# Attention and MoE on one core: where chunk 0's shifted V comes from, and the order of the first loads

## The chip, the cores and the metric

The kernel runs on one core of one Trainium2 chip. The metric is the device time of one execution in microseconds. Before the change the median of eight runs is 252.09 us (251.44 to 253.89). All other times in this document are from one profiled execution of the kernel, counted from the start of its span.

## The reference

Attention with two kinds of heads, followed by a two-layer network with a leaky ReLU:

```python
batch, n_heads, seq, head_dim = (4, 8, 768, 64)
n_sink, window = (4, 64)
is_retrieval = [1, 0, 1, 0, 0, 0, 1, 0]
n_tokens, d_model, d_ff = (3072, 512, 2048)

scores = scale * np.matmul(q, k.transpose(0, 1, 3, 2))
rel = pos[:, None] - pos[None, :]
causal = rel >= 0
stream_keep = causal & (is_sink | ((rel >= 0) & (rel < window)))
mask = full causal for retrieval heads, stream_keep for the others
a = softmax of the masked scores
attn_out = np.matmul(a, v)
x = attn_out, heads side by side           # 3072 x 512
h = x @ w_in
g = np.maximum(0.01 * h, h)
out = g @ w_out
```

Three heads of eight see the whole past. The other five ("stream" heads) see the last 64 keys and four first keys ("sinks").

## The kernel before

The 4 x 768 tokens are worked in eight chunks of 384; chunk n is batch n // 2, half n % 2. Each chunk goes through three stages: attention (class `Attention`, L289), the first matrix with the leaky ReLU (`in_slots`, L460, 16 slots of four matmuls), and the second matrix (`out_slots`, L472). `merge` (L503) lays the slots of one chunk's attention between matrix slots of the chunk before, and the order so written is the order in which every engine executes: nothing reorders it later. TensorE, ScalarE, VectorE, POOL and SP each run their own list in order, and meet at semaphores.

**Loads.** q, k, v and both weight matrices are float32 in DRAM and bfloat16 on the chip. A load that changes the type is issued by POOL (`load`, L78; `load_w`, L95). So POOL carries one long list of casting loads: q of chunk 0 (three), the identity matrix, v of chunk 0 (three), the masks (`masks`, L143), four loads of the first weights, then k, q and v of chunk 1, four loads of the second weights, and k, q, v of chunk 2 and on. The built program gives these loads eight completion semaphores in turn, so that each waits, on POOL, for the load eight places before it to have landed. k of chunk 0 comes by SP, without a cast.

**k and q with the head's width in the partitions.** Chunks 0 and 1 are transposed on TensorE (`prep_first`, L239; `prep_pair`, L205). From chunk 2 on SP issues six DMA transposes for each chunk (`prep_dma`, L228: `kt` from `kz` at L235, `qt` from `qb` at L237). SP's list in order is: shift of V for chunk 1, transposes of chunk 2, three stores of chunk 0's output, shift of V for chunk 2, transposes of chunk 3, and so on. Chunk 2's first score reads all of `qt`.

**Shifted V.** A stream head's query block of 64 needs 128 keys that begin 64 before it, so its V is read from `vb`, which holds V moved by 64 tokens. In most chunks SP makes `vb` from `va` by two DMA copies (`v_shift`, L176). In chunk 0 TensorE does it: `v_shift_pe` (L184) multiplies `va` with two shift matrices, four matmuls of 455 columns into the banks "py" and "pt", and ScalarE and VectorE copy one result each. `late_constants` (L157) builds the shift matrices and the mask of the stream heads, inside `prep_first`, ahead of the copy of q.

**Banks.** PSUM has eight banks: two "ph", two "psS", two "po", one "py", one "pt" (L55). A pair of heads accumulates in a "po" bank until VectorE has divided it (`finish`, L402); the result goes through a transpose bank (`x_t`, L417). An output tile of `out_slots` takes "py", which is free again when VectorE has copied it.

**The start** (L516 to L558) issues the loads, runs chunk 0's attention with `v_shift_pe` between slots 6 and 7, then seven in-slots of chunk 0, the four TensorE preparations of chunk 1 with an in-slot behind each, and the merge of the remaining in-slots and the out-slots of chunk 0 with chunk 1's attention.

Of the kernel before, what the change touches and what calls it, by code (L numbers as in the profile page):

```python
# [11 lines left out]
FP32 = mybir.dt.float32  # L12
BF16 = mybir.dt.bfloat16
ACTF = mybir.ActivationFunctionType
# [7 lines left out]
def kernel(  # L22
# [12 lines left out]
    nc = tc.nc  # L35
    B, H, S, D = q.shape
# [20 lines left out]
    def bank(tag, shape, dtype):  # L57
        return ps.tile(shape, dtype, name=tag, tag=tag, bufs=BANKS[tag])
# [19 lines left out]
    def load(n, nms="kqv"):  # L78

        b, c = divmod(n, 2)  # L80
        for nm in nms:
            if nm == "k" and n >= BY_DMA:

                for g in range(3):
                    for hh in range(2):
                        nc.gpsimd.dma_start(out=kz[n % 2][:, g, hh::2, D * hh : D * hh + D],  # L86
                                            in_=nat[nm][b, c, :, hh::2, g])
                continue
            if nm != "v":
                cast[nm, n] = rot.tile([128, 3, H, D], BF16, name=f"{nm}b", tag=f"{nm}b", bufs=2)  # L90
            for g in range(3):
                o = va[b % 2][:, 3 * c + g, :, 0:D] if nm == "v" else cast[nm, n][:, g]
                nc.gpsimd.dma_start(out=o, in_=nat[nm][b, c, :, :, g])  # L93

    def load_w(which, i):  # L95

        if which == "in":
            c = slice(512 * i, 512 * i + 512)
            nc.gpsimd.dma_start(out=w_in_bf[:, :, c], in_=w_in_r[:, :, c])
        else:  # L100
            c = slice(4 * i, 4 * i + 4)
            nc.gpsimd.dma_start(out=w_out_bf[:, c, :], in_=w_out_r[:, c, :])
# [5 lines left out]
    def bf(name, *shape):  # L108
        return one.tile([128, *shape], BF16, name=name)

    ident = bf("ident", 128)
    m_caus = bf("m_caus", 128)
    m_win0 = bf("m_win0", 6, 64)
    shift = bf("shift", 2, 128)
    kt = [bf(f"kt{i}", 4, 2, S) for i in range(2)]
    va = [bf(f"va{i}", 6, H, D + 1) for i in range(2)]
    vb = [bf(f"vb{i}", 5, H, D + 1) for i in range(2)]
# [25 lines left out]
    def masks():  # L143
        nc.gpsimd.memset(m_caus[:], 1.0)
        keep(m_caus[:], [[1, 128]], ALU.is_ge, 0, -1)
        nc.gpsimd.memset(m_w[:], 1.0)
        keep(m_w[:], [[-1, 64]], ALU.is_gt, 0, 1)
        keep(m_w[:], [[1, 64]], ALU.is_ge, 64, -1)

        nc.gpsimd.memset(m_h[:], 1.0)  # L150
        keep(m_h[:], [[-NS, H]], ALU.is_ge, 0, 1)
        keep(m_h[:], [[NS, H]], ALU.is_ge, NS - 1, -1)
# [2 lines left out]
        return ap.rearrange("p (o r) -> p o r", o=1).to_broadcast([128, n, w])  # L155

    def late_constants():  # L157

        nc.vector.tensor_copy(shift[:, 0, 0:64], ident[:, 64:128])
        nc.vector.tensor_copy(shift[:, 1, 64:128], ident[:, 0:64])  # L160
        nc.vector.tensor_copy(m_win0[:, 1:], spread(m_w[:], 5, 64))
        nc.vector.tensor_copy(m_win0[:, 0, :], m_caus[:, 0:64])
        nc.vector.memset(m_win0[0:NS, 1, :], 1.0)
        for h in range(H):
            if IS_RETR[h]:
                nc.vector.memset(m_h[:, h : h + 1], 0.0)
# [14 lines left out]
        eng.dma_start(out=vb[i][0:64, lo:hi], in_=va[i][64:128, lo:hi])  # L181
        eng.dma_start(out=vb[i][64:128, lo:hi], in_=va[i][0:64, lo + 1 : hi + 1])

    def v_shift_pe():  # L184

        w = 7 * (D + 1)
        for t in range(2):
            p = bank(("py", "pt")[t], [128, 512], FP32)
            for e in range(2):
                nc.tensor.matmul(p[:, 0:w], lhsT=shift[:, e, :], rhs=va[0][:, t + e, 1:H, :],  # L190
                                 start=(e == 0), stop=(e == 1))
            src = p[:, 0:w].rearrange("p (h d) -> p h d", h=7)
            if t == 0:
                nc.scalar.activation(out=vb[0][:, t, 1:H, :], in_=src, func=ACTF.Copy)
            else:
                nc.vector.tensor_copy(vb[0][:, t, 1:H, :], src)

    def sink_keys(n, p, hh):
        b, c = divmod(n, 2)
# [39 lines left out]
    def prep_first():  # L239

        k0 = stage["k"].rearrange("p h (g d) -> p g h d", g=3)
        qts[0] = rot.tile([128, 4, CH], BF16, name="qt", tag="qt", bufs=2)
        nc.vector.tensor_copy(cast["k", 0][:, :, 0:4], k0[:, :, 0:4])
        nc.scalar.activation(out=cast["k", 0][:, :, 4:8], in_=k0[:, :, 4:8], func=ACTF.Copy)
        pts = {}
        for nm, half, tag in (("k", 0, "pt"), ("k", 1, "py"), ("q", 0, "po"), ("q", 1, "po")):
            pt = pts[nm, half] = bank(tag, [128, 2, 4, 128], BF16)
            if nm == "q":
                continue
            for e in range(2):  # L250
                p = 2 * half + e
                for g in range(3):
                    nc.tensor.transpose(pt[:, e, g, :], cast[nm, 0][:, g, 2 * p : 2 * p + 2, :], ident[:])
        for g in range(3):
            for p in range(4):
                nc.tensor.transpose(pts["q", p // 2][:, p % 2, g, :], cast["q", 0][:, g, 2 * p : 2 * p + 2, :], ident[:])
        tok = lambda ap: ap.rearrange("p e (t g) -> p e t g", g=3)

        def k_rows(half, hh, act=False):
            ps2 = slice(2 * half, 2 * half + 2)  # L260
            r = slice(64 * hh, 64 * hh + 64)
            src = pts["k", half][r, :, 0:3, :].rearrange("p e g t -> p e t g")
            dst = tok(kt[0][r, ps2, hh, 0:CH])
            if act:
                nc.scalar.activation(out=dst, in_=src, func=ACTF.Copy)
            else:
                nc.vector.tensor_copy(dst, src)

        def q_rows(half):
            return (qts[0][:, 2 * half : 2 * half + 2, :].rearrange("p e (g t) -> p e g t", g=3),  # L270
                    pts["q", half][:, :, 0:3, :])

        k_rows(0, 0)
        k_rows(0, 1)
        k_rows(1, 0, True)
        k_rows(1, 1)
        for h in range(H):
            sink_keys(0, h // 2, h % 2)
        late_constants()
        d, r = q_rows(0)  # L280
        nc.scalar.activation(out=d, in_=r, func=ACTF.Copy)
        d, r = q_rows(1)
        nc.vector.tensor_copy(d, r)
# [174 lines left out]
    py = {}  # L458
# [13 lines left out]
    def out_slots(n, tags=("py", "py", "py"), halves=False):  # L472
        slots = []

        def part(tt, lo, hi, tag, c0, c1):
            if lo == 0:
                py[n] = bank(tag, [128, 512], FP32)
            for ng in range(lo, hi):
                nc.tensor.matmul(py[n][:, 0 : c1 - c0], lhsT=gs[n][:, ng, 128 * tt : 128 * tt + 128],  # L479
                                 rhs=w_out_bf[:, ng, c0:c1], start=(ng == 0), stop=(ng == NG - 1))  # L480
            if hi == NG:
                o = rot.tile([128, DM], FP32, name="o", tag="o", bufs=3)
                r0 = CH * n + 128 * tt
                nc.vector.tensor_copy(o[:, 0 : c1 - c0], py[n][:, 0 : c1 - c0])  # L484
                nc.sync.dma_start(out=out[r0 : r0 + 128, c0:c1], in_=o[:, 0 : c1 - c0])

        for tt in range(3):
            if halves and tt == 2:
                slots.append(lambda: part(2, 0, NG, "py", 0, 256))
                slots.append(lambda: part(2, 0, NG, "psS", 256, 512))  # L490
                continue
            lo = 0
            for w in ([3, 3, 3, 3, 4], [3, 3, 3, 3, 4], [3, 3, 3, 3, 2, 2])[tt]:
                slots.append(lambda tt=tt, lo=lo, w=w: part(tt, lo, lo + w, tags[tt], 0, DM))
                lo += w
        return slots

    def run(*lists):
        for l in lists:
            for f in l:  # L500
                f()

    def merge(ms, as_):  # L503

        r, done = [], 0
        for j, m in enumerate(ms):
            want = (j + 1) * len(as_) // len(ms)
            r += as_[done:want] + [m]
            done = want
        return r + as_[done:]  # L510
# [10 lines left out]
            nc.scalar.dma_start(out=sv[NS * h : NS * h + NS], in_=v[:, h, 0:NS, :].rearrange("b r d -> r b d"))  # L521
    for t in va:
        nc.vector.memset(t[:, :, :, D], 1.0)
    nc.vector.memset(shift[:], 0.0)
    zeros(0, 0)
    nc.vector.memset(ksink[0][:], 0.0)
    load(0, "v")
    masks()
    for i in range(4):
        load_w("in", i)  # L530
    load(1)
    for a in ats:
        nc.vector.memset(a[:, :, 1:3, :], 0.0)
    for i in range(4):
        load_w("out", i)
    prep_first()
    a0 = Attention(0, ("psS", "ph"), x_tags=("pt", "py")).slots(order=[0, 2, 1, 3, 4, 5, 6, 7], LAG=4, XLAG=3, sink_after={0, 2})
    run(a0[0:6])
    sink_values(0)
    v_shift_pe()  # L540
    run(a0[6:])
    zeros(0, 1)
    nc.vector.memset(ksink[1][:], 0.0)
# [2 lines left out]
    in0 = in_slots(0, ("ph", "psS"))  # L546
# [5 lines left out]
    prep_dma(2)  # L552

    a1 = Attention(1, po_tags=("po", "po", "po", "ph")).slots(order=[0, 2, 6, 1, 3, 4, 5, 7])
    run(merge(in0[11:], a1[:8]) + merge(out_slots(0), a1[8:]))
    zeros_k(1)
    v_shift(2, nc.sync)
    load(3)  # L558
# [58 lines left out]
```

The softmax here doesn't subtract the row's maximum and nothing guards it: scores larger than these inputs give would overflow.

## Time and profile before

| | |
|---|---|
| median of the runs | 252.09 us |
| profiled execution | 251.44 us, span 249.6 us |
| TensorE matmuls (PE) busy | 228.8 us, 92% |
| ScalarE (ACT) busy | 137.1 us, 55% |
| VectorE (DVE) busy | 86.7 us, 35% |
| POOL busy | 79.8 us, 32% |
| POOL's casting loads, as a share of 16 DMA engines | 70.8% |
| SP's and ScalarE's loads, copies, transposes and stores, the same share | 35.4% |

A row of the timeline gives start, length, engine (a "q" behind it means the engine's list of instructions that issue DMAs), line, operation, tile written <- tiles read, shape and count; in square brackets stands how long the engine sat idle before it, and what ended that. TensorE is busy in most of the span, but the idle time is not spread evenly: the start has nearly all of it. A row of DMA gives the issue; when the data landed is told beside it.

### The profile page before, as it was taken

Reading aid. Unit: us, or ns where it says so; the run is one execution under the profiler, and the core shown is the slowest. Engines: PE = TensorE matmul, PEld = TensorE weight load, DVE = VectorE, ACT = ScalarE, POOL = GpSimd, SP = SyncE. Lnnn points to the kernel's source line nnn. Section 1 sums busy time; section 2 is a strip of 40 time slices with the busy share of each in tenths; the row PEclk is TensorE's granted clock in tenths of the full one; section 3 lists DMA queues with packets and bytes.
Section 4 is the critical chain, followed back from the end, with each engine's and each line's share of the span. In section 5 each row is a group of like instructions: output and inputs, shape, how many; then the busy total and the mean of one; then the engine's idle time right before and its main releaser. Section 6 shows DMA issues by size and latency. Waiting matters only on the chain.

```text
span 249.6 us, 5031 instructions
## 1 busy us (share of the span) xinstructions
PE 228.8 (92%) x2012; PEld 138.5 (56%) x2012; DVE 86.7 (35%) x250; ACT 137.1 (55%) x297; POOL 79.8 (32%) x109
## 2 busy tenths in 40 slices
PE   1787799986999999989999999999999999999994
PEld 0564455553665567555665566566655566545553
DVE  6976141165235324323421323433521251111121
ACT  2665357433882298856556677556557667433300
POOL 8973833976437482385271000000000000000000
PEclk9999899999999999999999999999999999999999
DMA  9999999999999999999999921196100100111012
GB/s 163 125 204 180 166 234 181 138 166 189 213 135 160 184 200 139 162 120 151 197 169 194 135 67 42 49 146 145 45 27 19 42 20 25 42 45 42 28 56 87
DMA packets 110971, 30.14 MB, mean 121 GB/s; under 512 B 101732, under 2 KB 107108, under 8 KB 110948
## 3 DMA queue, kind: packets, MB, share of 16 engines
q0 software_dynamic: 76272, 13.24, 70.8%
q1 hardware_dynamic: 34576, 16.56, 35.4%
q8 instruction: 16, 0.26, 0.4%
q14 instruction: 7, 0.06, 0.1%
q10 hardware_dynamic: 100, 0.02, 0.0%
HBM read 27.28 MB, written 6.29 MB: 135 GB/s over the span
## 4 chain that ended last, share of the span: by engine, by line
PE 66%; DMA 22%; POOL 4%; SPq 3%; issue 2%; ACT 1%; DVE 1%; POOLq 0%
PE ph L466 26%; PE py L479 23%; DMA qb<-in_q_dram 8%; DMA qt<-qb 7%; DMA va<-in_v_dram 4%; PE po L308 4%; PE psS L341 4%; PE psS L479 3%; DMA w_in_bf<-in_moe_w_in_dram 3%; SPq L235 2%; POOL qb L93 2%; PE psS L377 2%; PE psS L466 1%; POOL va L93 1%; PE pt L420 1%
## 5 line engine op out<-in xcount | busy, mean ns | idle before, releaser
L466 PE MATMUL ph<-xt,w_in_bf 128*128 128x384 bf16 x480 | 97.2, 328 | 0.1
L479 PE MATMUL py<-w_out_bf,g 128*128 128x512 bf16 (+1 forms) x336 | 87.2, 374 | 1.5 <-DVE o L484 1.2
L468 ACT ACTIVATE g<-ph 128x384 bf16<-128x384 f32 x120 | 59.0, 492 | 49.2 <-PE ph L466 48.6
L466 PEld LDWEIGHTS <-w_in_bf 128*128 128x128 bf16 x512 | 45.9, 98 | 29.3 <-issue 1.5
L479 PEld LDWEIGHTS <-g 128*128 128x128 bf16 x400 | 35.7, 97 | 28.6 <-issue 2.9
L346 ACT ACTIVATE at<-psS 128x384 bf16<-128x384 f32 x81 | 39.2, 492 | 15.4 <-PE psS L341 14.3
L86 POOL DMA_DIRECT2D kz<-in_k_dram x36 | 26.8, 759 | 28.7 <-DMA kt<-kz 10.3
L341 PE MATMUL psS<-qt,kt 128*128 128x384 bf16 (+2 forms) x104 | 26.5, 295 | 2.6 <-DMA qt<-qb 2.2
L484 DVE COPY o<-py 128x512 f32<-128x512 f32 (+1 forms) x21 | 14.2, 677 | 40.4 <-PE py L479 40.2
L93 POOL DMA_DIRECT2D qb<-in_q_dram x24 | 21.3, 893 | 15.4 <-DMA va<-in_v_dram 8.0
L93 POOL DMA_DIRECT2D va<-in_v_dram x24 | 21.2, 897 | 6.9 <-DMA w_in_bf<-in_moe_w_in_dram 4.7
L382 ACT ACTIVATE ats<-psS 128x384 bf16<-128x384 f32 x38 | 18.8, 495 | 6.1 <-PE psS L377 6.0
L421 ACT ACTIVATE xt<-pt 128x384 bf16<-128x384 bf16 x30 | 14.7, 489 | 11.2 <-PE pt L420 10.7
L308 PE MATMUL po<-va,at 128*128 128x65 bf16 x237 | 20.3, 196 | 0.3 <-DVE at L350 0.3
L308 PEld LDWEIGHTS <-at 128*128 128x128 bf16 x252 | 16.4, 99 | 6.9 <-DVE at L350 0.7
L414 DVE TENSOR_TENSOR xs<-po,linv 128x384 bf16<-128x384 f32 x31 | 17.3, 558 | 1.1
L352 DVE TENSOR_TENSOR at<-at,m_caus 128x128 bf16<-128x128 bf16 x24 | 5.4, 225 | 34.5 <-ACT at L346 34.5
L341 PEld LDWEIGHTS <-kt 128*128 128x128 bf16 x108 | 10.5, 100 | 11.7 <-issue 4.9
L350 DVE TENSOR_TENSOR at<-at,m_caus 128x256 bf16<-128x256 bf16 x24 | 7.0, 291 | 24.4 <-ACT at L346 24.4
L377 PEld LDWEIGHTS <-kt 128*128 128x128 bf16 x240 | 12.1, 100 | 5.8 <-issue 0.7
L308 PE MATMUL po<-va,ats 128*128 128x65 bf16 x137 | 12.9, 194 | 1.1 <-DVE xs L414 1.1
L308 PEld LDWEIGHTS <-ats 128*128 128x128 bf16 x240 | 11.5, 98 | 3.9 <-DVE xs L414 1.2
(94 smaller groups left out, 176.2 us busy)
## 6 DMA issues: line engine op xcount, KB each, us to landing
out_dram<-o SPq DMA_DIRECT2D x23, 256.0 KB, 3.0
qb<-in_q_dram POOLq DMA_DIRECT2D x24, 128.0 KB, 8.1
va<-in_v_dram POOLq DMA_DIRECT2D x24, 128.0 KB, 10.2
kz<-in_k_dram POOLq DMA_DIRECT2D x36, 64.0 KB, 10.7
w_in_bf<-in_moe_w_in_dram POOLq DMA_DIRECT2D x4, 512.0 KB, 8.2
w_out_bf<-in_moe_w_out_dram POOLq DMA_DIRECT2D x4, 512.0 KB, 12.0
vb<-va SPq DMA_DIRECT2D x8, 195.0 KB, 5.9
vb<-va SPq DMA_DIRECT2D x6, 130.0 KB, 4.1
```

Of the source, the lines that this page charges most:

```text
L86: nc.gpsimd.dma_start(out=kz[n % 2][:, g, hh::2, D * hh : D * hh + D], in_=nat[nm][b, c, :, hh::2, g])
L93: nc.gpsimd.dma_start(out=o, in_=nat[nm][b, c, :, :, g])
L308: nc.tensor.matmul(o, lhsT=lhsT, rhs=rhs, start=first, stop=False, skip_group_check=True)
L341: nc.tensor.matmul(s[:, off : off + w], lhsT=kt[i][:, p, hh, 128 * kj : 128 * kj + 128], rhs=qts[n][:, p, lo:CH], start=(j == 0), stop=(j ...
L346: nc.scalar.activation(out=a[:, 0:off], in_=s[:, 0:off], func=ACTF.Exp, scale=SM)
L377: nc.tensor.matmul(s[:, 64 * m : 64 * m + 64], lhsT=kt[i][:, p, hh, k0 : k0 + 128], rhs=qts[n][:, p, 64 * m : 64 * m + 64], start=(m == 0) ...
L382: nc.scalar.activation(out=av_, in_=s[:, 0:CH].rearrange("p (j e f) -> p j e f", j=3, e=2), func=ACTF.Exp, scale=SM)
L414: nc.vector.tensor_tensor(xs[:], po[:, :, :, 0:D], linv.to_broadcast([128, 3, 2, D]), op=ALU.mult)
L421: nc.scalar.activation(out=xts[self.n][:, p, :], in_=pt[:, 0, 0:3, :], func=ACTF.Copy)
L466: nc.tensor.matmul(ph[:, 0:CH], lhsT=w_in_bf[:, g, 128 * t : 128 * t + 128], rhs=xts[n][:, g, :], start=(g == 0), stop=(g == KG - 1))
L468: nc.scalar.activation(out=gs[n][:, t, :], in_=ph[:, 0:CH], func=ACTF.Prelu, alpha=0.01)
L479: nc.tensor.matmul(py[n][:, 0 : c1 - c0], lhsT=gs[n][:, ng, 128 * tt : 128 * tt + 128], rhs=w_out_bf[:, ng, c0:c1], start=(ng == 0), stop= ...
```

## The change

Four things are changed, all of them in the first two chunks:

- `v_shift_pe` and its shift matrices are gone. `load_vb0` loads the first two blocks of chunk 0's shifted V from DRAM by two casting loads on POOL, behind v and ahead of the masks. Their column of ones is set by one memset, in place of the one that cleared the shift matrices.
- Chunk 0's attention uses "py" as a third accumulator bank (pair 2), and "pt", "ph", "psS", "pt" for its transposes. Chunk 0's out-slots use "py", "ph", "py".
- `late_constants` is called behind the first four slots of chunk 0's attention.
- k and q of chunk 1 are loaded ahead of the fourth load of the first weights; v of chunk 1 stays behind it.

```diff
-    shift = bf("shift", 2, 128)
...
     def late_constants():
-
-        nc.vector.tensor_copy(shift[:, 0, 0:64], ident[:, 64:128])
-        nc.vector.tensor_copy(shift[:, 1, 64:128], ident[:, 0:64])
         nc.vector.tensor_copy(m_win0[:, 1:], spread(m_w[:], 5, 64))
...
-    def v_shift_pe():
...
+    def load_vb0():
+
         for t in range(2):
...
+            nc.gpsimd.dma_start(out=vb[0][:, t, :, 0:D],
+                                in_=v[0, :, 128 * t + 64 : 128 * t + 192, :].rearrange("h p d -> p h d"))
...
             sink_keys(0, h // 2, h % 2)
-        late_constants()
         d, r = q_rows(0)
...
-    nc.vector.memset(shift[:], 0.0)
+    nc.vector.memset(vb[0][:, 0:2, :, D], 1.0)
     zeros(0, 0)
     nc.vector.memset(ksink[0][:], 0.0)
     load(0, "v")
+    load_vb0()
     masks()
-    for i in range(4):
+    for i in range(3):
         load_w("in", i)
-    load(1)
+    load(1, "kq")
+    load_w("in", 3)
+    load(1, "v")
...
-    a0 = Attention(0, ("psS", "ph"), x_tags=("pt", "py")).slots(order=[0, 2, 1, 3, 4, 5, 6, 7], LAG=4, XLAG=3, sink_after={0, 2})
-    run(a0[0:6])
+    a0 = Attention(0, ("psS", "ph"), po_tags=("po", "po", "py", "po"),
+                   x_tags=("pt", "ph", "psS", "pt")).slots(order=[0, 2, 1, 3, 4, 5, 6, 7], LAG=4, XLAG=3, sink_after={0, 2})
+    run(a0[0:4])
+    late_constants()
+    run(a0[4:6])
     sink_values(0)
-    v_shift_pe()
     run(a0[6:])
...
-    run(merge(in0[11:], a1[:8]) + merge(out_slots(0), a1[8:]))
+    run(merge(in0[11:], a1[:8]) + merge(out_slots(0, ("py", "ph", "py")), a1[8:]))
```

## The prediction, made before the changed kernel was run

> **What bounds the kernel now.** I read the page's chain and busy shares first, then the TensorE groups that sat idle, then the queues that the chain names (SP and POOL), and last the granted clock by stretches of 3.4 us. TensorE's rows with idle time before them, for the stretch 60 to 130 us, are only four:
>
> ```profile
> 61.39 0.32 PE L341 MATMUL psS<-qt,kt 128*128 128x384 bf16 x1 [1.45 <-DMA qt<-qb]
> 102.68 0.27 PE L308 MATMUL po<-va,at 128*128 128x65 bf16 x3 [0.30 <-DVE at L350]
> 104.75 0.34 PE L420 MATMUL pt<-ident,xs 128*128 128x128 bf16 x3 [0.23 <-DVE xs L414]
> 107.16 0.32 PE L341 MATMUL psS<-qt,kt 128*128 128x384 bf16 x1 [0.77 <-DMA qt<-qb]
> ```
>
> From 61.39 us to the end TensorE stands still for 0.30 + 0.23 + 0.77 = 1.3 us. So the end is set by when chunk 2's first score (61.39) may start, plus TensorE work that this change leaves alone. That score waits for a DMA, not for TensorE: SP's queue shows the six transposes of chunk 2 (start, issue time),
>
> ```profile
> 43.53 1.37 SPq L235 DMA_TRANSPOSE kt<-kz  x1
> 46.11 1.19 SPq L237 DMA_TRANSPOSE qt<-qb  x1
> 47.41 1.49 SPq L235 DMA_TRANSPOSE kt<-kz  x1
> 49.00 1.78 SPq L237 DMA_TRANSPOSE qt<-qb  x1
> 50.88 2.73 SPq L235 DMA_TRANSPOSE kt<-kz  x1
> 53.70 1.42 SPq L237 DMA_TRANSPOSE qt<-qb  x1
> ```
>
> and the chain follows the last for 7.55 us, to 61.25. The first needs two kz loads; those were issued at 29.13 and 30.19 and took 13.9 and 13.3 us to land: 43.0 and 43.5. They are late because POOL's queue is full ahead of them: the page's DMA row is at nine tenths or more from the start to slice 23. POOL's own rows show where that queue begins:
>
> ```profile
> 4.62 2.75 POOL L93 DMA_DIRECT2D va<-in_v_dram  x3
> 7.34 0.24 POOL L144 MEMSET m_caus<- 128x128 bf16 x1
> ...
> 8.77 0.45 POOL L128 TENSOR_SCALAR_AFFINE_SELECT m_h<-m_h 128x8 bf16<-128x8 bf16 x2
> 9.16 3.01 POOL L99 DMA_DIRECT2D w_in_bf<-in_moe_w_in_dram  x4
> ```
>
> The bound of the front, then, is POOL's queue of casting loads -> kz and q of chunk 2 -> transposes -> 61.39. TensorE's own work before 61 us has slack: it was done at 61.39 - 1.45 = 59.94.
>
> **The change, part by part.**
>
> *Two loads of shifted V on POOL, ahead of the masks.* They have the shape of the va loads (128 partitions x 8 heads x 64 values). The nearest row is L93, va<-in_v_dram, 897 ns of POOL each: 2 x 0.897 = 1.79 us. Behind them on POOL stand the masks and every later load. Masks first: m_caus is ready at 7.95 + 1.79 = 9.7, needed at about 11 by the first mask product; m_w and m_h at about 11, needed by the moved constants later still. Nothing is lost there. Then the weights: the first w_in load goes from 9.16 to 10.95. It took 5.6 us to land (14.74), the next three landed at 17.25, 19.8 and 23.3 (7.3, 9.1 and 11.9 us after issue). From there the queue has no gap until w_out has landed, so all that stands behind w_in, kz of chunk 2 included, shifts by 1.79.
>
> Here a rule speaks for a smaller number. The Trainium skill, "DMA: Bandwidth & Descriptors", section "Anatomy of one DMA — SWDGE (gpsimd) path", puts a software-queue transfer at a fixed 2.0 us of completion plus bytes/436e3; the fixed part overlaps in a full queue, so two loads of 256 KB read would cost 2 x 0.6 = 1.2 us. The rows here disagree: three va loads took 2.75 us of POOL, and chunk 1's three q loads reached TensorE at 27.11, 28.01 and 28.89, 0.9 us apart. By the rule the shift is 1.2, by the rows 1.8. I take the rows, and keep 1.2 as the lower end.
>
> *k and q of chunk 1 ahead of the fourth w_in load.* TensorE stood still for q three times (to 27.11, 28.01, 28.89). The fourth w_in load held the queue from 19.8 to 23.3 = 3.5 us, so the last q lands at 28.84 + 1.79 - 3.5 = 27.1, a gain of 1.7 us at that place. The fourth w_in load then lands at about 30.6; its first user (in-slot 12) ran at 36.0. v of chunk 1, w_out and kz have the same loads ahead of them as before plus two: +1.79. Nothing of the gain reaches them.
>
> *V shift taken off TensorE.* Four 455-column matmuls from 13.21 to 14.71 go (1.5 us), with one ScalarE copy of 0.55 us and one VectorE cast of 0.63. In their place the first vb product waits for the loads: issued at about 7.4 and 8.2, with the 5.1 us that va loads took they land at 12.5 and 13.4; the first use stood at 15.91 and may come at 14. Wait 0 to 0.5 us. The vb ones memset replaces the shift memset (0.17 us): nothing.
>
> *Constants later, third bank.* VectorE's constants (10.69 to 11.55, 0.86 us) now stand behind four mask products; chunk 0's second q copy comes 0.9 earlier, which the 0.26 us wait at 12.17 pays back. The bank "py" for pair 2 removes the wait of 1.09 us at 17.93. Together TensorE is through chunk 0 some 2 to 3 us earlier (21.4 -> about 18.7), and all of it is lost to the wait for q at 27.1.
>
> *What TensorE makes of it up to 61 us.* It leaves the q wait 1.7 us earlier. Next in its way is w_out: the four loads landed at 33.7, 37.8, 40.0 and 42.6 (8.0, 11.4, 12.6, 14.3 us after issue), now 1.79 later; the last, 44.4, is needed by the out-slot that started at 44.85 and would now start at 43.1. So 0.5 us of the gain is left. Chunk 0's output banks py, ph, py instead of py alone remove the two waits for the output copy (0.53 at 46.66, 0.68 at 53.29): 1.2 us. TensorE is done with what it can do at 59.94 - 0.5 - 1.2 = 58.2. The gate comes at 61.25 + 1.79 = 63.0. Everything saved on TensorE becomes idle time there: 4.8 us where it was 1.45. **The start of chunk 2 moves by +1.8 us.**
>
> *The granted clock.* The price of such a gap is in the trace of before (columns: stretch, length, busy us of PE, PEld, DVE, ACT and POOL, granted PE clock, DMA share, GB/s):
>
> ```profile
> 25.51:28.93 3.42, 1.56 (x12) 0.79 (x11) 0.00 (x0) 1.10 (x3) 3.11 (x5) 1.00 2.43 155
> 28.93:32.34 3.41, 3.41 (x17) 2.07 (x18) 2.13 (x6) 0.49 (x1) 2.51 (x5) 0.50 1.54 193
> 59.65:63.06 3.41, 1.97 (x14) 1.10 (x13) 2.24 (x9) 1.48 (x4) 1.81 (x3) 1.00 1.60 241
> ```
>
> After a stretch with 1.56 us of TensorE in 3.42 the clock was halved for 3.41 us, which costs 1.7 us of dense matmuls; after one with 1.97 us it was not. The Trainium skill, "TensorE: Matmul & The Clock Gate", Part 1, says that the clock falls to half after an idle window of about 3.4 us, the windows running free of the program. Read literally, a 4.8 us gap holds a whole window in (4.8 - 3.4)/3.4 = 4 of 10 phases: 0.4 x 1.7 = 0.7 us. The row shows that a window half idle, with a few transposes in it, is enough; with 4.8 us some window is at least 2.4 us idle in any phase. I take the row: one window, +1.7 us (0, or up to 3 where a second window is needed to rise again, are the ends).
>
> *What is given back.* Chunk 4's transposes start behind chunk 1's output copies on SP, so behind TensorE, and move with it; but the loads they compete with do not wait for the cold clock, so half of the 0.77 us at 107.16 may go: -0.4.
>
> Sum: 1.8 + 1.7 - 0.4 = **+3.1 us**. The profiled execution took 251.44 us (span 249.6 and 1.84 around it), the fastest of eight; it becomes 254.5. The median of the runs, 252.09, becomes **255.2 us**.
>
> **Rivals.**
>
> *Gate late, clock kept.* The gap is shorter than I think (w_out later, TensorE later), or falls well in the windows. +1.8: 253.9. For it: the gap at 61.39 was not punished before. Against: all TensorE savings lengthen it.
>
> *No change.* The two loads fit into the hole that the masks leave in the DMA queue (in 10.0 to 11.3 us the queues moved 24 GB/s against 151 in 5 to 10). Against: w_in's issue, not the engines, ended that hole, and it moves too. It needs a shift under 1.2 us: about 252.5.
>
> *Faster: the transposes shed their competition.* The six took 43.53 to 61.25 = 17.7 us beside the casting loads; the six of chunk 7, from 160.77, with POOL idle, landed 3.3 us (kt) and 2.5 us (qt) after issue in the median, the last, issued at 167.89, by 170.3: 9.6 us. If the new order spaced the loads so that the transposes ran 3.1 us faster, the gate would fall under 59.9 and TensorE's savings would count: 58.4 at best, -3 us, 249. It decides from 17.7 - 3.1 = 14.6 us on. Against: the loads beside the transposes are the same, shifted with them.
>
> *Two windows cold, or a slower transpose group:* +4.5 to 5, 257.
>
> **How the numbers follow.** Late and cold 0.53 (255.2, own range 254.0 to 256.8), late and warm 0.20 (253.9), no change 0.14 (252.5), faster 0.07 (249), worse 0.06 (257). A measurement here tells about 0.5% (1.3 us) from no change. Faster 0.07; within 0.5%, 0.16, with a piece of the warm case that comes out below 253.35; slower 0.77. The range leaves out the faster case and the tail above: 252.4 to 257.0.
>
> **What would show it.** Right: w_in's first issue at about 11, last q of chunk 1 at TensorE at about 27, the first transpose on SP at about 45.3, chunk 2's first score near 63 behind 4 us or more of waiting for qt, then a stretch of 3.4 us at clock 0.50. Wrong: a first transpose at 43.5 or earlier, or a last one landing before 61; or a score that waits for TensorE. If the first transpose moves and the end does not, the transposes' own rate is the step that failed.

## The result, and the profile after

The changed kernel takes 256.59 us (median of 11 runs, 255.34 to 257.66) where the kernel before, run beside it, takes 252.46 us: 1.0157 times as long, 95% interval 1.0128 to 1.0186. (Ratios, here and below, leave out runs more than 1.5% above the fastest of the same kernel, so that they need not equal the ratio of the medians.) That is +4.1 us where +3.1 was forecast (255.2, range 252.4 to 257.0). The profiled execution has a span of 254.9 us, 5.3 more than the one before.

TensorE's rows with idle time before them, from 60 to 130 us:

```profile
65.31 0.48 PE L328 MATMUL psS<-qt,kt 128*128 128x384 bf16 x1 [6.81 <-DMA qt<-qb]
108.96 0.26 PE L295 MATMUL po<-va,at 128*128 128x65 bf16 x3 [0.30 <-DVE at L337]
111.03 0.34 PE L407 MATMUL pt<-ident,xs 128*128 128x128 bf16 x3 [0.23 <-DVE xs L401]
```

Chunk 2's first score starts at 65.31 instead of 61.39, and TensorE stood still for 6.81 us ahead of it instead of 1.45. Behind it only 0.53 us is idle: the wait at 107.16 is gone. SP's six transposes that the score waits for:

```profile
46.00 1.33 SPq L223 DMA_TRANSPOSE kt<-kz  x1
48.52 1.19 SPq L225 DMA_TRANSPOSE qt<-qb  x1
49.83 1.41 SPq L223 DMA_TRANSPOSE kt<-kz  x1
51.34 2.07 SPq L225 DMA_TRANSPOSE qt<-qb  x1
53.52 4.12 SPq L223 DMA_TRANSPOSE kt<-kz  x1
57.73 1.50 SPq L225 DMA_TRANSPOSE qt<-qb  x1
```

The first starts 2.5 us later than before; the chain follows the last to 65.17, so the group takes 19.2 us instead of 17.7. POOL's rows show the delay at its source:

```profile
4.39 0.86 POOL masks.py:199 TENSOR_SCALAR_AFFINE_SELECT ident<-ident 128x128 bf16<-128x128 bf16 x1
5.20 2.67 POOL L93 DMA_DIRECT2D va<-in_v_dram  x3
7.84 1.78 POOL L183 DMA_DIRECT2D vb<-in_v_dram  x2
9.57 0.26 POOL L143 MEMSET m_caus<- 128x128 bf16 x1
...
11.51 2.27 POOL L99 DMA_DIRECT2D w_in_bf<-in_moe_w_in_dram  x3
```

The two V loads hold POOL for 1.78 us (their row has no bracket: POOL waited for nothing). The first w_in load is issued at 11.51, 2.35 later than before: 1.78 of it are the loads, 0.57 the identity matrix's row, which is taken up again below. The granted clock by stretches (columns: stretch, length, busy us of PE, PEld, DVE, ACT and POOL, granted PE clock, DMA share, GB/s):

```profile
56.50:59.91 3.41, 1.42 (x10) 0.65 (x8) 1.90 (x7) 1.47 (x3) 1.92 (x3) 1.00 2.02 142
59.91:65.31 5.40, 0.00 (x1) 0.03 (x1) 0.18 (x2) 0.00 (x0) 4.12 (x5) 0.50 1.68 188
65.31:70.15 4.84, 4.84 (x17) 2.43 (x18) 0.52 (x2) 2.02 (x5) 1.33 (x2) 0.50 1.40 245
70.15:73.50 3.35, 3.35 (x33) 2.27 (x32) 0.97 (x3) 2.51 (x6) 0.89 (x2) 1.00 1.69 156
```

The clock fell to half (a "cold" clock) in the gap and stayed there until 70.15, so 4.84 us of dense matmuls ran at half speed: 2.4 us lost. The row ahead of it, 56.50 to 59.91, is taken up again below. Sum for this pair of profiles: 3.92 (start of chunk 2) + 2.42 (clock) - 0.77 (the wait at 107) = 5.6 us, where the spans differ by 5.3; 0.3 us the other way is not accounted for.

### The profile page after: what moved, and what is told of

It is laid out like the page before. It is cut to its first block, busy times and chain, and to the rows that moved or that the text cites. A ratio compares the mean times of both kernels' runs of the same rounds, so it can differ in the third digit from the quotient of the medians.

```text
span 254.9 us, 5020 instructions
## 1 busy us (share of the span) xinstructions
PE 230.5 (90%) x2008; PEld 139.7 (55%) x2008; DVE 85.9 (34%) x247; ACT 137.0 (54%) x296; POOL 82.1 (32%) x111
## 4 chain that ended last, share of the span: by engine, by line
PE 71%; DMA 16%; POOL 8%; issue 1%; DVE 1%; ACT 1%; SPq 0%; POOLq 0%
PE ph L453 28%; PE py L466 24%; DMA w_out_bf<-in_moe_w_out_dram 6%; PE po L295 5%; PE psS L328 4%; DMA w_in_bf<-in_moe_w_in_dram 4%; PE psS L466 3%; DMA kz<-in_k_dram 3%; POOL va L93 3%; DMA qt<-qb 3%; PE psS L364 2%; POOL qb L93 2%; PE pt L407 2%; PE ph L466 1%; PE psS L308 1%
## 5 line engine op out<-in xcount | busy, mean ns | idle before, releaser
L453 PE MATMUL ph<-xt,w_in_bf 128*128 128x384 bf16 x480 | 99.4, 333 | 0.1
L466 PE MATMUL py<-w_out_bf,g 128*128 128x512 bf16 (+1 forms) x320 | 83.0, 374 | 0.9 <-DMA w_out_bf<-in_moe_w_out_dram 0.7
L453 PEld LDWEIGHTS <-w_in_bf 128*128 128x128 bf16 x512 | 46.6, 99 | 30.7 <-issue 3.6
L471 DVE COPY o<-py 128x512 f32<-128x512 f32 (+1 forms) x20 | 13.5, 677 | 41.2 <-PE py L466 41.1
L401 DVE TENSOR_TENSOR xs<-po,linv 128x384 bf16<-128x384 f32 x30 | 16.7, 557 | 1.0
L364 PE MATMUL psS<-qt,kt 128*128 128x64 bf16 x228 | 13.2, 196 | 0.0
```

The costliest lines, as they stand in the source:

```text
L364: nc.tensor.matmul(s[:, 64 * m : 64 * m + 64], lhsT=kt[i][:, p, hh, k0 : k0 + 128], rhs=qts[n][:, p, 64 * m : 64 * m + 64], start=(m == 0) ...
L401: nc.vector.tensor_tensor(xs[:], po[:, :, :, 0:D], linv.to_broadcast([128, 3, 2, D]), op=ALU.mult)
L453: nc.tensor.matmul(ph[:, 0:CH], lhsT=w_in_bf[:, g, 128 * t : 128 * t + 128], rhs=xts[n][:, g, :], start=(g == 0), stop=(g == KG - 1))
```

## The experiments

Theory 1 is that of the prediction: the two loads put every later POOL load back, with them kz and q of chunk 2 and the transposes, and what TensorE saves turns into a longer gap and a cold clock. Against it stand: the new order of k, q and w_in or the banks are to blame; the loads fit into a hole of the queues; the cold clock costs nothing.

### The two loads alone

The kernel before with one part of the change:

```diff
     load(0, "v")
+    load_vb0()
     masks()
...
-    v_shift_pe()
```

> The kernel before with one part of the change: shifted V of chunk 0 by two casting loads on POOL instead of TensorE; order of loads, constants and banks as before. Theory 1 (the two loads delay all that POOL loads behind them, and with it the transposes of chunk 2): first transpose on SP at 45.3 to 46.0, first score of chunk 2 at 63 to 65.3, TensorE idle before it 1.5 to 3.5 us (nothing is saved on TensorE), so 254.3 to 256.5. Rival (the new order of k, q and w_in, or the banks, are to blame): first transpose at 43.5, 252.5.

Measured: 255.31 us, 1.0073 times the kernel before (1.0042 to 1.0104). SP's first transpose:

```profile
45.75 1.33 SPq L223 DMA_TRANSPOSE kt<-kz  x1
```

and TensorE's first score of chunk 2:

```profile
64.01 0.32 PE L329 MATMUL psS<-qt,kt 128*128 128x384 bf16 x1 [1.53 <-DMA qt<-qb]
```

With the loads alone the transposes start 2.2 us and the score 2.6 us later than in the first profile of the kernel before; 0.6 us of both is the identity matrix's row, not the loads. The gap is not longer than before (1.53), since TensorE is late too: it waited for q until 31.00. The group of transposes hardly grew: 18.1 us instead of 17.7, with 2.71 us for the third kt as before (2.73):

```profile
52.86 2.71 SPq L223 DMA_TRANSPOSE kt<-kz  x1
```

In this profile no cold clock follows the gap. That the loads by themselves make the kernel slower is shown; order and banks are not needed for it.

### Everything but the two loads

The changed kernel with V shifted on TensorE again:

```diff
-    load_vb0()
     masks()
...
     sink_values(0)
+    v_shift_pe()
     run(a0[6:])
```

> The changed kernel with that one part undone: shift of V on TensorE again; order, constants and banks as changed. Theory 1: first transpose back at 43.5, first score of chunk 2 at 61.4. TensorE is ready some 3 us earlier than before, so the gap there is 4 to 5 us and the clock goes cold behind it: 252.5 + 1.7 to 2.4 - 0.4 = 254.1; with a warm clock 252.4. Rival (order or banks are to blame): 256.6.

Measured: 253.52 us, 1.0038 (1.0011 to 1.0065). The first score:

```profile
62.52 0.48 PE L340 MATMUL psS<-qt,kt 128*128 128x384 bf16 x1 [6.00 <-DMA qt<-qb]
```

and the stretch of TensorE work behind it, in the columns of the stretches above:

```profile
62.52:68.45 5.93, 5.93 (x23) 2.92 (x24) 0.52 (x2) 2.35 (x5) 1.48 (x2) 0.50 1.44 230
```

The transposes start at 43.83, near the 43.5 expected. The score comes 1.1 us later than the 61.4 expected, since the group took 18.6 us instead of 17.7; the third kt took 3.75 us:

```profile
50.96 3.75 SPq L235 DMA_TRANSPOSE kt<-kz  x1
```

The three parts that help TensorE (third bank, early q, output banks) bring it to the gap at 56.52, 3.4 us earlier than in the first profile of the kernel before, which waits 1.45 us there; here it waits 6.00 us, the clock goes cold, and 5.93 us of matmuls run at half speed. Work saved ahead of a gap that another engine ends has made the kernel slightly slower.

### V shifted by two SP copies

```diff
-    load_vb0()
+    v_shift(0, nc.sync)
     masks()
```

> The changed kernel with chunk 0's shifted V copied from va by two SP copies, as later chunks have it, so neither POOL nor TensorE pays. Theory 1: vb lands near 18, TensorE waits 2 to 3 us for it in chunk 0, hidden behind the wait for q; first transpose at 43.5 to 44.2, first score at 61.4 to 62, 252.5 to 254.5. Rival (loads from DRAM are not the point, any shift off TensorE leaves a long gap before chunk 2): 256 or more.

Measured: 255.28 us, 1.0107 (1.0079 to 1.0135), above the range of theory 1. TensorE's wait in chunk 0, and the first score of chunk 2:

```profile
18.69 0.19 PE L289 MATMUL po<-vb,ats 128*128 128x65 bf16 x1 [3.85 <-DMA vb<-va]
...
63.79 0.48 PE L322 MATMUL psS<-qt,kt 128*128 128x384 bf16 x1 [5.92 <-DMA qt<-qb]
```

The wait in chunk 0 came (3.85 us, 2 to 3 expected) and was hidden. The miss is in the transposes: the first started at 45.32, not 43.5 to 44.2. POOL's first w_in load was issued at 9.60, as without V loads (9.69). But its second landed at 18.95, where it was 17.65 in the run without the two loads; the fourth, which goes out 0.28 us behind that landing in both runs, was issued at 19.23 instead of 17.93, and the two kz loads of the first transpose had landed at 45.26 instead of 43.77. The two copies are all that SP and POOL move in addition up to there, so they put the loads back by about 1.3 us; that they do so by taking time of the same DMA engines is likely, and not shown. That the copies cost nothing was wrong. The rival, that any V shift off TensorE leaves a long gap, asked for 256 us or more: the time lies between the two, the gap is long, and it comes with later transposes.

### The old order of w_in, k and q

```diff
-    for i in range(3):
+    for i in range(4):
         load_w("in", i)
-    load(1, "kq")
-    load_w("in", 3)
-    load(1, "v")
+    load(1)
```

> The changed kernel with the order of the loads of before (all four w_in, then k, q, v of chunk 1), the two V loads kept. Theory 1: last q of chunk 1 at 30.6 to 31.5 instead of 28.1, but kz lands as in the changed kernel, first score of chunk 2 at 65.3; TensorE gets there 2 us later, so the gap is 3 to 5 us; 254.5 to 256.6. Rival (k and q ahead of the fourth w_in are to blame): first score at 61.4 to 63, 252.5 to 254.

Measured: 255.87 us, 1.0097 (1.0062 to 1.0133). The first score of chunk 2:

```profile
65.28 0.48 PE L328 MATMUL psS<-qt,kt 128*128 128x384 bf16 x1 [4.36 <-DMA qt<-qb]
```

The first score is where the changed kernel has it, with TensorE 2.4 us later at the gap. The order of k and q moves only TensorE's arrival: it is not to blame for the late score, and it brings nothing. The old order may even be a little faster (1.0097 beside 1.0157); the intervals just touch.

### The gap filled with matmuls

The changed kernel with 36 matmuls in the gap, whose result nobody reads:

```diff
+    warm = bank("pt", [128, 512], FP32)
+    for j in range(36):
+        nc.tensor.matmul(warm[:, 0:CH], lhsT=ident[:], rhs=w_in_bf[:, 0, 0:CH], start=(j == 0), stop=(j == 35))
     run(merge(in_slots(1) + out_slots(1, ("py", "ph", "py")), Attention(2).slots()))
```

> The changed kernel with 36 extra matmuls of 384 columns (about 5.9 us, their result is not used) just before chunk 2's first slots, in the time in which TensorE waits for qt. Theory (the gap is paid twice, once as waiting and once as a cold clock behind it): first score still at 65.3, no half-clock stretch from 60 to 70 us, so the 2.4 us that the clock cost are gone: 254.2. Rival (the clock costs nothing, the loads set the pace behind 65 us too): 256.6. Filling lasting longer than the gap: above 256.6.

Measured: 254.29 us, 1.0068 (1.0045 to 1.0091), where the theory gave 254.2. The first score:

```profile
64.78 0.32 PE L328 MATMUL psS<-qt,kt 128*128 128x384 bf16 x1 [0.28 <-DMA qt<-qb]
```

and the stretch behind it:

```profile
64.78:70.20 5.42, 5.42 (x46) 3.61 (x47) 1.49 (x5) 4.62 (x11) 1.21 (x2) 1.00 1.79 226
```

The score starts within 0.5 us of where it was, behind a gap of 0.28, and the clock is full: 46 matmuls in 5.42 us. In every run of the changed kernel the mean granted clock was 0.970 to 0.980, in the 22 runs of this one 0.986 to 0.998. Doing more work made the kernel 2.3 us faster. That is about what the cold clock costs the changed kernel; how much of the 4.1 us it explains depends on what it costs the kernel before, see below.

### Two more loads

The changed kernel with two further loads of the same shape, into a tile that nobody reads:

```diff
     load_vb0()
+    for t in range(2):
+        nc.gpsimd.dma_start(out=spare[:, t], in_=v[0, :, 128 * t + 64 : 128 * t + 192, :].rearrange("h p d -> p h d"))
     masks()
```

> The changed kernel with two more casting loads of the same shape and source into a tile that nobody reads, right behind the two of the change. Theory 1 (each such load costs 0.9 us of POOL and so of all that is queued behind it): w_in's first issue at 13.3 instead of 11.5, first transpose on SP at 47.8, first score at 67, 258.4. Rival (the loads fit into a hole of the DMA queues, the delay has another cause): first transpose at 46, 256.6.

Measured, in four runs: 258.03 us, 1.0196 (1.0129 to 1.0264). The spare loads and the first w_in load on POOL:

```profile
9.57 1.80 POOL L518 DMA_DIRECT2D spare<-in_v_dram  x2
...
13.32 0.77 POOL L99 DMA_DIRECT2D w_in_bf<-in_moe_w_in_dram  x1
```

SP's first transpose:

```profile
47.56 1.33 SPq L224 DMA_TRANSPOSE kt<-kz  x1
```

and the first score:

```profile
67.64 0.48 PE L329 MATMUL psS<-qt,kt 128*128 128x384 bf16 x1 [7.59 <-DMA qt<-qb]
```

1.80 us on POOL became 1.81 at w_in, 1.56 at the first transpose, 2.33 at the score. There is no hole that takes the loads in.

### kz and q of chunk 2 earlier

The kernel without the V loads (TensorE shifts V) and with three moves on POOL; one third of kz and q is loaded by `load_kq`:

```diff
     load(0, "v")
-    masks()
     for i in range(3):
         load_w("in", i)
+    masks()
...
-    for i in range(4):
+    for i in range(3):
         load_w("out", i)
...
     zeros_k(0)
-    load(2)
+    load_kq(2, 0)
+    load_w("out", 3)
+    load_kq(2, 1)
+    load_kq(2, 2)
+    load(2, "v")
```

> Shift of V on TensorE as before, the other parts of the change kept, and three moves on POOL: the masks behind the first three w_in loads, the first third of kz and q of chunk 2 ahead of the fourth w_out load, and kz and q of chunk 2 in turns. Theory (POOL's queue up to kz and q sets the start of chunk 2): first transpose at 40 to 41, last qt landed by 58 to 59, first score at 58 to 59 instead of 61.4, gap under 2 us, clock warm; 249 to 251, less what chunk 4's transposes at 107 take back. Rival (the transposes' own rate sets it, whatever the loads): 252.5 to 253.5.

Measured: 251.31 us, 0.9936 (0.9908 to 0.9964): faster than both kernels, 0.3 us above the 249 to 251 expected ahead of what chunk 4's transposes give back. SP's first transpose:

```profile
40.37 1.35 SPq L245 DMA_TRANSPOSE kt<-kz  x1
```

and TensorE's wait for w_out and its first score of chunk 2:

```profile
43.65 1.26 PE L488 MATMUL py<-w_out_bf,g 128*128 128x512 bf16 x4 [2.10 <-DMA w_out_bf<-in_moe_w_out_dram]
60.66 0.32 PE L350 MATMUL psS<-qt,kt 128*128 128x384 bf16 x1 [1.79 <-DMA qt<-qb]
```

The transposes start 3.2 us earlier than in the first profile of the kernel before, but take 20.2 us instead of 17.7, so the score, expected at 58 to 59, gains only 0.7 us on that profile (2.2 on its second, below). The cold clock is not there behind the gap. So each theory is half right: POOL's queue sets when the transposes start, and their rate beside the casting loads takes most of the gain back. The price of the early loads, 2.10 us of waiting for w_out and a half clock behind that wait (44.29 to 47.71), is hidden.

### The same with the two V loads

```diff
     load(0, "v")
     load_vb0()
-    masks()
     for i in range(3):
         load_w("in", i)
+    masks()
```

and the moves at `load(2)` as above.

> The changed kernel, its two V loads kept, with the same three moves on POOL. Theory: everything behind the two loads is 1.8 us later than without them: first transpose at 42 to 43, first score at 60 to 61, 251 to 253. Rival (with the moves the loads are hidden): same as without the two loads.

Measured: 253.22 us, 1.0017 (0.997 to 1.0065), 0.2 us above the range expected. SP's first transpose:

```profile
42.10 1.34 SPq L233 DMA_TRANSPOSE kt<-kz  x1
```

and the first score:

```profile
62.14 0.32 PE L338 MATMUL psS<-qt,kt 128*128 128x384 bf16 x1 [1.49 <-DMA qt<-qb]
```

First transpose 1.73 and score 1.48 us later than without the loads: their price again, in a kernel whose profile has the full clock behind the gap (its half clock, 45.99 to 49.40, is behind the wait for w_out). The score came 1.1 us later than expected, for the reason of the run above.

### A second profile of both kernels

> The kernel before, unchanged, for a second profile. If 0.6 us of the difference between the two profiles is chance (POOL's identity mask took 0.29 us in the profile before and 0.86 us in every other one, and all its loads start behind it): 0.86 us here too, w_in's first issue at 9.7, first transpose at 43.8 to 44.2, first score of chunk 2 at 61.5 to 62.5. If it belongs to the kernel: 0.29 us, 9.16, 43.5 and 61.4 again. Time 251 to 254 either way.

> The changed kernel, unchanged, for a second profile: first transpose at 45.5 to 46.2, first score of chunk 2 at 64 to 65.5, half clock behind it for 3.4 to 10.2 us, of which TensorE feels 1 to 5 us. Time 255.3 to 257.7.

Single executions: 254.79 us for the kernel before, 257.40 for the changed one. Of the kernel before, on POOL, first the row of the first profile, then that of the second:

```profile
4.38 0.29 POOL masks.py:199 TENSOR_SCALAR_AFFINE_SELECT ident<-ident 128x128 bf16<-128x128 bf16 x1
```

```profile
4.38 0.90 POOL masks.py:199 TENSOR_SCALAR_AFFINE_SELECT ident<-ident 128x128 bf16<-128x128 bf16 x1
```

its first score of chunk 2:

```profile
62.87 0.48 PE L341 MATMUL psS<-qt,kt 128*128 128x384 bf16 x1 [4.01 <-DMA qt<-qb]
```

and the stretch behind that:

```profile
62.87:68.82 5.95, 5.95 (x24) 2.95 (x25) 0.52 (x2) 2.34 (x5) 1.85 (x3) 0.50 1.62 227
```

The identity matrix takes 0.90 us here: the 0.29 of the first profile was chance, and with it 0.6 us of the difference between the first two profiles. (0.29 came again in the profiles of the two kernels below.) First transpose at 44.09 and score at 62.87, the latter 0.4 past the range expected, and the time 0.8 past it. More: this execution has no cold clock at 29 us, comes to the gap earlier, waits 4.01 us in place of 1.45, and then runs 5.95 us at half clock. Over many runs the kernel before splits in the same way. Of the 59 runs beside the first experiments 27 had a mean granted clock of 0.984 to 0.987, as this one (0.987), and a median of 254.3 us; the other 32 had 0.990 to 0.993, as the first profile (0.993), and 251.6. (3.41 us at half clock lower the mean of such a run by 0.007; where in a run they lay is known for the profiled ones alone.) The second profile of the changed kernel is like its first, its score 0.2 past the range expected:

```profile
65.66 0.48 PE L328 MATMUL psS<-qt,kt 128*128 128x384 bf16 x1 [7.57 <-DMA qt<-qb]
```

Pair by pair, the score is 3.9 us (first profiles) and 2.8 us (second) later.

### Ten matmuls in the gap of the kernel before, and of the faster one

The same filler with `range(10)`.

> The kernel before with 10 extra matmuls of 384 columns (1.6 us, result not used) ahead of chunk 2's first slots, in its gap of 1.5 to 4 us. Theory (the spread of the kernel before, 250.7 to 254.7, comes from whether the clock is cold behind the gap): the upper part of the spread goes, median 251.2 to 252.2. Rival (the spread has another cause): 252.5 to 253.2, since the matmuls only take waiting time, or add up to 0.2.

> The kernel with kz and q of chunk 2 loaded early, with the same 10 extra matmuls in its gap of 1.8 us. Theory: no half clock behind the gap in any execution, 249.5 to 250.8. Rival (its gap is too short to be punished): 251.3.

Measured: 251.62 us for the first, 0.9969 (0.9937 to 1.0001), with a highest run of 253.22 where the kernel before beside it had a median of 252.85 and reached 254.83; 250.26 us for the second, 0.9926 (0.9894 to 0.9958), the fastest kernel of this study. Its score:

```profile
59.30 0.32 PE L350 MATMUL psS<-qt,kt 128*128 128x384 bf16 x1 [1.25 <-DMA qt<-qb]
```

The median of the first is in the range that the theory gave, and none of its 14 runs had a mean clock under 0.991, where 13 of the 29 of the kernel before had 0.984 to 0.987. But the interval touches 1, and the two slowest of the filled runs, 253.18 and 253.22, had the full clock (1.000). So the cold clock is a part of the spread, and not all of it; the identity matrix's 0.6 us may be another. In the second, the step from 0.9936 to 0.9926 is smaller than either interval; whether the filler adds to the early loads stays open.

With this filler the parts of the change can be set apart. With both gaps filled, the changed kernel stands at 1.0068 and the kernel before at 0.9969: the late start costs about 2.5 us. The clock costs the changed kernel 2.3 us and the kernel before 0.8, so it adds about 1.5 us. By the intervals each of these is good to about 1 us, and ten matmuls may not fill the longer gaps of the kernel before.

## Why the prediction was right

The direction, the place and the mechanism held. The sum came within a microsecond, but by terms that were each too small and partly cancel: that it came so close is in part luck.

- **Two loads on POOL, +1.8 us.** Right: 1.78 in the profile, 1.80 for two more. The smaller figure of 1.2 us from the rule on software-queue transfers did not hold. The first transpose moved by 2.5 in the first pair of profiles, of which 0.57 was the identity matrix's chance, and by 1.6 in the second pair (45.69 against 44.09).
- **The transposes keep their rate.** Mis-sized: the term "the gate comes at 61.25 + 1.79 = 63.0" took the group at 17.7 us. It took 19.2 and 19.8 in the changed kernel, 17.7 and 18.6 in the kernel before. So the score moved 3.9 and 2.8 us instead of 1.8. The later place in the queue does little of this: with the two loads alone the group took 18.1 us, with everything but the loads 18.6. The third kt, 4.12 us in the changed kernel, tells the same: about 2.7 in both profiles of the kernel before and with the loads alone, 3.75 without the loads. So most of the longer group goes with the parts that were to help TensorE; what in them does it was not tried.
- **k and q earlier, banks, V off TensorE: nothing reaches the end.** Right that nothing is gained; that the gate stays where the loads put it is the step just named. q's last piece met TensorE at 28.14, a microsecond later than worked out, and w_out made it wait for 0.67 us at 44.94. Its savings became gap: 6.81 us instead of the 4.8 forecast, because the transposes were later than thought and TensorE was ready at 58.5. The run without the loads (1.0038, 1.0011 to 1.0065) shows that they cost time.
- **A cold clock behind the gap, +1.7 us.** Right in kind, mis-sized: 2.4 us in the profile, 2.3 by the filled gap. "One window" was three, 10.24 us, of which TensorE met 4.84. And the prediction took for granted that the kernel before pays nothing here. Its second profile lost 3.0 us, and by the two fillers the clock's share of the difference is about 1.5 us: near the 1.7, because two errors cancel. The choice of the row over the literal reading of the rule held: the clock fell at 59.91, at the end of a stretch with 1.42 us of TensorE in 3.41, when only 1.41 us of the gap were over. With the old order of the loads it fell at 62.30 behind 1.45 us of work in 3.41, where the next 3.41 us are not wholly idle either (the gap there ends at 65.28).
- **-0.4 given back at 107 us.** The whole 0.77 went. The second profile of the kernel before does not have this wait.

In the first pair of profiles: 3.9 + 2.4 - 0.8 in place of 1.8 + 1.7 - 0.4. In the second: 2.8 for the start, 2.3 (4.69 us at half clock) - 3.0 for the clock, 2.1 us in all, where the times differ by 2.6.

Of the rivals, "gate late, clock kept" is the kernel with the two loads alone in its profile; "no change" fell with the result, and its hole in the queue with the two more loads. "Faster, the transposes shed their competition" went the other way in every run: no group whose end is seen took less than 17.7 us.

## What to carry to other kernels

Before work is taken off the busiest engine, find the next place where it waits for something else, and ask what the edit does to that. Here two loads of 0.9 us each on a full issue queue delayed a start that came more than 50 us behind them. TensorE's earlier arrival at that place (1.4 us in the first pair of profiles, 3.4 without the V loads) bought nothing but a longer gap, whose cold clock cost the changed kernel 2.3 us. The edit that helped moved what the gap was waiting for ahead of loads that had slack.

## What was not expected of the hardware

A cold clock ahead of a gap can be free, and can even spare one behind it. In the first profile of the kernel before, the clock was at half from 28.93 to 32.34; TensorE came later to the gap at 61 us, waited 1.45, and went on at full speed, 251.44 us in all. In the second the clock was full there; TensorE came early, waited 4.01, and lost 3.0 us to the half clock behind the gap, 254.79 us in all. The same program and inputs: the kernel before ranges over 250 to 255 us. This is read from one pair of profiles, which differ in the identity matrix's 0.6 us too; no run tested it. Where the gap is long it does not help: the changed kernel had the half clock from 29.18 to 32.60 as well, and again behind its 6.81 us.

The Trainium skill ("TensorE: Matmul & The Clock Gate", Part 1) says that the windows in which activity is judged run free of the program, which fits, and that a busy window brings the clock back: in the changed kernel the half clock lasted three windows of 3.41 us (59.91 to 70.15), with TensorE silent in the first, at work for the last 1.4 us of the second, and in all of the third. A window in which TensorE worked for 1.4 us brought nothing back, and in the stretch before (56.50 to 59.91) as much work had not kept the clock up.
